# Where the folded down weights are stored, and where the first raw weights are placed, in a spectral layer with a gated feed-forward on one core

## The chip, the cores and the metric

The kernel runs on one core of a Trainium2 chip. The metric is the device time of one execution in microseconds, as the median of several runs. The core's engines are PE (matrix products), DVE (vector operations), ACT (activations and copies), POOL (a second, slower vector engine) and SP, whose queue issues most of the transfers. Each engine works through its own instructions strictly in order and waits at the head of its queue for whatever the next instruction needs.

## The reference

The input x has 4096 rows of 640 values. A modulation vector (six pieces of 640: sa, ca, ga, sb, cb, gb) is computed from c.

```python
mod = (_silu(c) @ w_mod).reshape(c.shape[0], 6, 1, -1)
h = _layernorm(x) * (1 + ca) + sa
x = x + ga * _A_ref(h, ...)          # FFT over the rows, a two-layer block-diagonal net, inverse FFT
h = _layernorm(x) * (1 + cb) + sb
x = x + gb * ((_silu(h @ w_gate) * (h @ w_up)) @ w_down)   # 640 -> 1728 -> 640
```

Everything is float32. The kernel keeps that accuracy by splitting an operand into a high and a low part and adding three products (high·high, high·low, low·high).

## The kernel before

The first 313 us compute the spectral layer A. The rest is the feed-forward layer, to which the change belongs. Its 32 groups of 128 rows are cut into six tiles t = 0 to 5 (`TL`, of 4, 4, 6, 6, 6 and 6 groups). For each tile PE runs a fixed list of stages `STG`: weight blocks of gate and up (`w`, 14 of them, n = 0 to 13) and, in between, the down products of six pairs of blocks (`d`, p = 0 to 5; the remainder p = 6, called `NPR`, is used together with p = 5).

The order of all other work is made by a planner in the kernel's Python code, when the program is built. PE's stages move the planner's clock `now` on by assumed durations. Every other piece of work is a `Step`: an engine letter (A for ACT, V for DVE, P for POOL, S for SP's queue, N for nothing), an assumed duration, a function that issues the instructions, the keys it depends on, the key it finishes, the places it takes (`use`) and the places it gives back (`free`). Steps stand in chains, and a chain's steps are issued strictly one after another. After every 0.3 us of assumed PE time `sweep` goes through all chains and issues each first step whose dependencies and places are planned to be there in time. A step on SP is planned to be issued 0.45 us after it is taken up, and its transfer to end 0.9 us + its duration + 0.9 us later, behind all transfers planned before it (`free["D"]`). Where the plan is early, the real engine waits at the instruction, and all that stands behind it on that engine waits too.

The chain `down_w` prepares the down weights. In tile 0, `prep_wd(0, p)` does for each p: `load` the raw block of 640 KB from `w_down` into the one place `wd`; `fold(0)` and `fold(1)` on POOL, which multiply it in place by the gate row gb (L1589); for each half the `high` part on ACT (L1594) into a place of `wdh` and the `low` part on DVE (L1598) into a place of `wdl` (two places each, given back when a down stage is through); and `store`, which writes the folded block to the scratch tensor `wdd` (L1601), from which later tiles load it (L1580) without folding. Before, `store` is the last step of the block and gives the place `wd` back; the next block's `load` takes it.

The raw gate and up blocks r (L1405) are loaded by `load_w`, the first three (n = 1, 2, 0) ahead of the first stage. Each is split into high parts (ACT, L1423) and low parts (DVE, L1426), and POOL makes differences of its quarters, `ts` (L1470), for later tiles. PE's first stage `first_g` uses weights that the spectral part has prepared already; beside it ACT and DVE split the first rows (L1887 to L1893). A row of the next tile goes through a chain of its own: loads of the spectral result `cr` and of `x` (L1638, L1634), a product with the gate row on POOL (L1650), a split (`chh`, `chl`, L1654 and L1657), an inverse transform on PE (L1667), statistics on DVE (L1678), scales on POOL (L1686 to L1689), the normalised row `xn` on ACT (L1698) and its transposes on PE (L1731).

`place` fixes at which address each kind of tile lies: addresses are given out in the order of the calls. The feed-forward's memory lies over that of the spectral part, so a first tile can be written only when the last reader of what lay there is through.

Of the kernel before, what the change touches and what calls it, by code (L numbers as in the profile page):

```python
# [6 lines left out]
F32 = mybir.dt.float32  # L7
# [6 lines left out]
P = 128  # L14
D = 640
S = 4096
# [155 lines left out]
def body(tc, x, w1, b1, w2, b2, wg, wu, wd, c, wm, k_fa, k_tb, k_tx, k_bm, k_bx, k_ga, k_ge, k_id, out, dbg=None):  # L172
# [4 lines left out]
    def f32(ap):  # L177
        return ap.bitcast(F32)
# [22 lines left out]
    with ExitStack() as top:  # L201
# [922 lines left out]
        with ExitStack() as ff:  # L1124
# [36 lines left out]
            free = dict.fromkeys("AVPSDG", 0.0)  # L1161
            done = {}
# [164 lines left out]
            def take(tag, shape, dt, bufs, name):  # L1327
                if tag == "wt":
                    turns[0] += 1
                    if turns[0] % 3 == 0:  # L1330
                        return low_p.tile(shape, dt, tag=tag, name=name)
                    bufs = 2
                if first.get(tag):
                    return first[tag].pop(0)
                return fp.tile(shape, dt, tag=tag, bufs=bufs, name=name)

            def place(tag, shape, dt, bufs, name):
                first.setdefault(tag, []).append(fp.tile(shape, dt, tag=tag, bufs=bufs, name=name))
# [6 lines left out]
            place("rb0", [P, 512], F32R, 1, "a13")  # L1345
            place("wt", [P, 2, 2, 2, P], F32R, 2, "wt0_0a")
            place("R", [P, 5, 256], F32, 2, "r0_2")
            ht0 = [fp.tile([P, 2, 512], F32R, tag=f"h{j}", bufs=1, name=f"ht0_{j}") for j in HT0]
            place("h0", [P, 4, 2, P], F32, 1, "ts0")
            place("h1", [P, 5, 256], F32, 1, "r0_1")  # L1350
            place("pc", [P, D], F32, 4, "cr0_0")
            place("px", [P, D], F32, 2, "x0_0")
            for f in range(2):
                for hl in range(2):
                    place(f"a{2 * f + hl}", [P, 512], F32R, 1, f"a0_0_{f}_{hl}")
            place("h32", [P, 5, 2, P], F32, 1, "h32_1_0")
            place("wd", [P, 2, D], F32, 1, "wdr0_0")
            place("wdh", [P, 2, D], F32R, 2, "wdh0_0")
            place("sg", [P, 512], F32, 4, "sg0_0_0")
            place("s", [P, 512], F32, 5, "hx0_0")  # L1360
# [30 lines left out]
            raw = {}  # L1391
# [6 lines left out]
            def load_w(t, n):  # L1398
                k, p = WG[n]
                tag = rtag(t, n)  # L1400

                def load():
                    r = raw[t, n] = take(tag, [P, 5, 256], F32, bufs[tag], f"r{t}_{n}")
                    if k in "gu":
                        nc.sync.dma_start(r, (wgv if k == "g" else wuv)[:, :, 256 * p:256 * p + 256])  # L1405
                    else:
                        c, f = (P, 12 * P) if k == "m" else (64, 13 * P)
                        nc.sync.dma_start(r[:, :, 0:c], wgv[:, :, f:f + c])
                        nc.sync.dma_start(r[:, :, c:2 * c], wuv[:, :, f:f + c])

                return Step("S", 2.1, load, key=("raw", t, n), use=(tag,))
# [86 lines left out]
            wds = {}  # L1498
# [74 lines left out]
            def prep_wd(t, p):  # L1573
                if t in DT:
                    return block_loads(t, p)

                def load():
                    w = wdraw[t, p] = take("wd", [P, 2, D], F32, 1, f"wdr{t}_{p}")
                    if t:
                        nc.sync.dma_start(w.rearrange("p a b -> p (a b)"), wdd[p])  # L1580
                    elif p < NPR:
                        nc.sync.dma_start(w, wd[256 * p:256 * p + 256, :].rearrange("(f p) d -> p f d", p=P))
                    else:
                        nc.sync.dma_start(w[:, 0], wd[12 * P:13 * P, :])
                        for h in range(2):
                            nc.sync.dma_start(w[64 * h:64 * h + 64, 1], wd[13 * P:F, :])

                def fold(f):
                    pool.tensor_tensor(wdraw[t, p][:, f], wdraw[t, p][:, f], gbb[0], op=OP.mult)  # L1589

                def high(f):
                    if f == 0:
                        wds[t, p] = [take(q, [P, 2, D], F32R, 2, f"{q}{t}_{p}") for q in ("wdh", "wdl")]
                    act.activation(wds[t, p][0][:, f], wdraw[t, p][:, f], AF.Copy)  # L1594

                def low(f):
                    h, l = wds[t, p]
                    dve.tensor_tensor(l[:, f], wdraw[t, p][:, f], f32(h[:, f]), op=OP.subtract)  # L1598

                def store():  # L1600
                    nc.sync.dma_start(wdd[p], wdraw[t, p].rearrange("p a b -> p (a b)"))  # L1601

                raw_ = ("wdr", t, p)
                out = [Step("S", 1.7, load, (("wds", p),) if t else (), raw_, ("wd",))]
                for f in range(2 if t == 0 else 0):
                    out += [Step("P", 1.65, lambda f=f: fold(f), (raw_, ("gbb", 0), ("gbb", 1)), ("wdg", p, f))]
                for f in range(2):
                    out += [Step("A", 0.74, lambda f=f: high(f), (raw_,) if t else (("wdg", p, f),), ("wdhh", t, p, f),
                                 () if f else ("wdh", "wdl")),
                            Step("V", 0.83, lambda f=f: low(f), (("wdhh", t, p, f),), ("wdf", t, p, f),  # L1610
                                 free=("wd",) if f and t else ())]

                if t == 0:
                    out.append(Step("S", 1.7, store, (("wdf", t, p, 0), ("wdf", t, p, 1)), ("wds", p), free=("wd",)))
                return out

            def wd_keys(t, p):
# [805 lines left out]
            for n in (1, 2, 0):  # L2423
                prep.add([load_w(0, n)])
                prep.run()
            for i in range(2):
                done["gbb", i] = done["wb", 0, 0, i] = 0.0

# [27 lines left out]
            for t in range(NT):  # L2456
                for p in (0, 1, NPR, 2, 3, 4, 5) if t in DT else range(NPR + 1):
                    down_w.add(prep_wd(t, p))
                if t >= NS:
                    for n in range(NW):  # L2460
                        if WG[n][0] != "s":
                            wtl.add([load_t(t, n, i) for i in range(2)])
                if t:
                    left_l.add(load_h(t))
                    x2_l.add(load_x2(t))
                    rows[t].add(row_chain(t))
# [55 lines left out]
```

## Time and profile before

| what | value |
|---|---|
| three timed runs | 1455.12, 1455.55, 1457.36 us, median 1455.55 |
| the profiled execution | 1462.3 us, its span 1460.5 us |
| mean granted clock of PE | 0.998 |
| PE busy | 1409.4 us, 97% of the span |
| DVE, ACT, POOL busy | 1091.5, 784.8, 537.9 us |
| HBM read, written | 264.04 MB, 104.86 MB |

All times of the profile are counted from the start of the span. A row of waits says which engine and line waited for which, how long in total, how often, and the longest. A row of a timeline begins with start and length. A row of the chain of work that ended last gives start, length and the work. "x6" counts instructions.

### The profile page before, as it was taken

What the parts mean: (1) busy time and instruction counts of PE and PEld (TensorE: products, weight loads), DVE (VectorE), ACT (ScalarE), POOL (GpSimd) and SP (SyncE); (2) the same over time, 40 slices, a digit from 0 to 9 for tenths busy, and PEclk for the clock granted to TensorE, in tenths of its full rate; (3) what the DMA queues carried; (4) which work ended last, traced back from release to release, by engine and by line L of the source; (5) the groups of instructions that cost most, each with busy time, mean ns of one, the idle gap of its engine ahead of it and who ended that gap; (6) DMA issues with size and microseconds to landing.
All of it is one profiled execution on the core that took longest, in us unless ns stands there. A gap on an engine that the chain in (4) does not pass through costs nothing.

```text
span 1460.5 us, 23931 instructions
## 1 busy us (share of the span) xinstructions
PE 1409.4 (97%) x8516; PEld 1329.9 (91%) x8516; DVE 1091.5 (75%) x1979; ACT 784.8 (54%) x1560; POOL 537.9 (37%) x640
## 2 busy tenths in 40 slices
PE   7999999999989989999999999999999999999998
PEld 2699999968879878899999999999999999999998
DVE  8878778869777888668878768788747767567775
ACT  7868878745454455545555456556434444244432
POOL 5300100146444234233444434534324545046532
PEclk9999999999999999999999999999999999999999
DMA  9987677647877977897886997888696666966652
GB/s 379 321 257 251 208 219 234 212 138 263 272 264 252 326 257 258 296 357 271 284 312 214 355 368 246 289 279 272 237 346 218 219 216 238 353 210 232 204 188 83
DMA packets 186807, 379.66 MB, mean 260 GB/s; under 512 B 22176, under 2 KB 104672, under 8 KB 184896
## 3 DMA queue, kind: packets, MB, share of 16 engines
q1 hardware_dynamic: 178496, 361.75, 72.2%
q0 software_dynamic: 6608, 13.77, 3.0%
q10 hardware_dynamic: 1584, 2.62, 0.5%
q8 instruction: 67, 1.10, 0.3%
q14 instruction: 52, 0.43, 0.1%
HBM read 264.04 MB, written 104.86 MB: 253 GB/s over the span
## 4 chain that ended last, share of the span: by engine, by line
PE 69%; DVE 11%; DMA 10%; ACT 4%; issue 2%; POOL 2%; SPq 1%; DVEq 0%; POOLq 0%; ACTq 0%
PE pd L2396 12%; PE pw L2075 7%; PE pw L2077 7%; PE pw L2076 7%; PE pd_X L2256 4%; PE pc L780 4%; PE pl L712 4%; DMA cr<-s 3%; PE pd_Y L2256 2%; PE pw L2086 2%; PE pw L2088 2%; PE pw L2087 2%; PE pg L1939 2%; PE pg L1940 2%; PE pg L1941 2%
## 5 line engine op out<-in xcount | busy, mean ns | idle before, releaser
L2396 PE MATMUL pd<-wdh,a 128*128 128x320 f32 x1040 | 240.2, 311 | 0.3 <-ACT sg L1961 0.3
L2396 PEld LDWEIGHTS pd<-wdh,a 128*128 128x128 f32 x1040 | 177.4, 189 | 0.9 <-ACT sg L1961 0.5
L1426 DVE TENSOR_TENSOR wb<-r,wb 128x512 fp32r<-128x512 f32 (+3 forms) x154 | 159.8, 1049 | 12.6 <-ACT wb L1423 10.4
L2396 PE MATMUL pd<-wdl,a 128*128 128x320 f32 x540 | 166.9, 310 | 0.0
L2075 PE MATMUL pw<-h,wt 128*128 128x384 f32 x416 | 141.2, 339 | 4.3 <-ACT s_x L2094 3.3
L2077 PE MATMUL pw<-h,wt 128*128 128x384 f32 x416 | 140.3, 337 | 0.0
L2076 PE MATMUL pw<-h,wt 128*128 128x384 f32 x416 | 139.7, 336 | 0.0
L2368 DVE TENSOR_TENSOR x<-x,pd 128x320 f32<-128x320 f32 x240 | 109.2, 478 | 38.3 <-PE pd L2396 34.3
L1423 ACT ACTIVATE wb<-r 128x512 fp32r<-128x512 f32 (+3 forms) x170 | 116.4, 704 | 30.7 <-PE pw L2088 23.3
L2075 PE MATMUL pw<-h,wb 128*128 128x384 f32 x312 | 105.2, 337 | 0.0
L2077 PE MATMUL pw<-h,wb 128*128 128x384 f32 x312 | 104.7, 336 | 0.0
L2076 PE MATMUL pw<-h,wb 128*128 128x384 f32 x312 | 104.6, 335 | 0.0
L1939 PE MATMUL pg<-ht,wb 128*128 128x512 f32 x260 | 102.8, 396 | 0.0
L1941 PE MATMUL pg<-ht,wb 128*128 128x512 f32 x260 | 101.7, 391 | 1.0 <-DVE wb L1426 1.0
L2396 PEld LDWEIGHTS pd<-wdl,a 128*128 128x128 f32 x540 | 102.0, 189 | 0.4
L1940 PE MATMUL pg<-ht,wb 128*128 128x512 f32 x260 | 101.7, 391 | 0.0
L2094 ACT ACTIVATE s_x<-pw 128x384 f32<-128x384 f32 x52 | 25.4, 489 | 114.0 <-PE pw L2077 113.3
L1650 POOL TENSOR_TENSOR cr<-cr,gab 128x640 f32<-128x640 f32 x28 | 47.5, 1697 | 101.4 <-DMA cr<-s 83.5
L2075 PEld LDWEIGHTS pw<-h,wt 128*128 128x128 f32 x416 | 78.1, 188 | 6.9 <-ACT s_x L2094 4.9
L842 POOL DMA_DIRECT2D s<-co x28 | 15.5, 555 | 181.9 <-ACT co L841 172.9
L2076 PEld LDWEIGHTS pw<-h,wt 128*128 128x128 f32 x416 | 78.2, 188 | 0.0
L2077 PEld LDWEIGHTS pw<-h,wt 128*128 128x128 f32 x416 | 78.1, 188 | 0.0
(353 smaller groups left out, 4049.5 us busy)
## 6 DMA issues: line engine op xcount, KB each, us to landing
wt<-td SPq DMA_DIRECT2D x104, 512.0 KB, 5.4
hs<-ho SPq DMA_DIRECT2D x52, 512.0 KB, 5.4
h<-hs SPq DMA_DIRECT2D x32, 768.0 KB, 8.5
r<-in_B_w_up_dram SPq DMA_DIRECT2D x36, 640.0 KB, 5.4
r<-in_B_w_gate_dram SPq DMA_DIRECT2D x36, 640.0 KB, 5.3
wdr<-wdd SPq DMA_DIRECT2D x21, 640.0 KB, 5.4
td<-wt SPq DMA_DIRECT2D x25, 512.0 KB, 5.7
g<-s SPq DMA_DIRECT2D x7, 1280.0 KB, 7.0
```

The costliest lines, as they stand in the source:

```text
L712: mm(pls[g][:, :NN], *seqs[g][i], start=(i == 0), stop=(i == n - 1))
L1423: act.activation(wbs[t, n][:, 0, ks, e], raw[t, n][:, ks, e], AF.Copy)
L1426: (pool if onp else dve).tensor_tensor(wbs[t, n][:, 1, ks, e], raw[t, n][:, ks, e], f32(wbs[t, n][:, 0, ks, e]), op=OP.subtract)
L1939: mm(b, wh, hh, start=(kk == 0), stop=False)
L1940: mm(b, wh, hl, start=False, stop=False)
L1941: mm(b, wl, hh, start=False, stop=(kk == 4))
L2075: mm(b, w(0, kp), a[:, kp, 0], start=start and kp == 0, stop=False, skip_group_check=not start)
L2076: mm(b, w(0, kp), a[:, kp, 1], start=False, stop=False, skip_group_check=not start)
L2077: mm(b, w(1, kp), a[:, kp, 0], start=False, stop=kp == 1, skip_group_check=not start)
L2256: mm(bk[b, i][:, :320], x, y, start=new and j == 0, stop=j == len(seq) - 1, skip_group_check=not new)
L2368: dve.tensor_tensor(x2[:, e], x2[:, e], x[0][:, :320], op=OP.add)
L2396: mm(pd[g, hf][0][:, :320], l, m, start=i == 0, stop=i == len(s) - 1 and not (last and len(gs) > 1))
```

## The change

Four edits. The store of a folded block becomes the fourth step of its block, right behind the second fold, with the two fold keys `("wdg", p, 0)` and `("wdg", p, 1)` as its dependencies in place of the low parts' keys; the high and low parts follow it in the chain. The place `wd` is given back by a new step of engine "N", which issues nothing and depends on the store's key and on the second low part. The place `h1` (the first raw up weights, `r0_1`) is given out ahead of the five tiles `ht0` in place of behind `h0`, and the place `wd` (the first raw down weights, `wdr0_0`) ahead of the tiles `a0` to `a3` in place of behind `h32`, which moves the tiles between by 5 to 6 KB per partition. And after the first three raw loads the planner is told that these blocks are there at time 0, and that SP's queue and the transfers are free at time 0.

```diff
             place("R", [P, 5, 256], F32, 2, "r0_2")
+            place("h1", [P, 5, 256], F32, 1, "r0_1")
             ht0 = [fp.tile([P, 2, 512], F32R, tag=f"h{j}", bufs=1, name=f"ht0_{j}") for j in HT0]
             place("h0", [P, 4, 2, P], F32, 1, "ts0")
-            place("h1", [P, 5, 256], F32, 1, "r0_1")
             place("pc", [P, D], F32, 4, "cr0_0")
             place("px", [P, D], F32, 2, "x0_0")
+            place("wd", [P, 2, D], F32, 1, "wdr0_0")
...
             place("h32", [P, 5, 2, P], F32, 1, "h32_1_0")
-            place("wd", [P, 2, D], F32, 1, "wdr0_0")
...
                 if t == 0:
-                    out.append(Step("S", 1.7, store, (("wdf", t, p, 0), ("wdf", t, p, 1)), ("wds", p), free=("wd",)))
+                    out.insert(3, Step("S", 1.7, store, (("wdg", p, 0), ("wdg", p, 1)), ("wds", p)))
+                    out.append(Step("N", 0.0, lambda: None, (("wds", p), ("wdf", t, p, 1)), free=("wd",)))
                 return out
...
             for n in (1, 2, 0):
                 prep.add([load_w(0, n)])
                 prep.run()
+                done["raw", 0, n] = 0.0
+            free["S"] = free["D"] = 0.0
```

## The prediction, made before the changed kernel was run

> **What bounds the kernel now.** I read the page first, then the waits of PE in the stretch that the edited steps fill, then the chain that ended last through it, then the granted clock around the largest wait.
>
> ```profile
> span 1460.5 us, 23931 instructions
> PE 1409.4 (97%) x8516; PEld 1329.9 (91%) x8516; DVE 1091.5 (75%) x1979; ACT 784.8 (54%) x1560; POOL 537.9 (37%) x640
> ```
>
> PE is busy for 97% of the span, so its 51.1 us of idle time (1460.5 - 1409.4) are all that a change of order can win. The folds lie between 313 and 460 us. The waits of PE there (total, times, longest):
>
> ```profile
> PE pt L1731 <- ACT xn L1698: 3.5, 1, 3.5
> PE py L1667 <- DVE chl L1657: 2.8, 2, 1.6
> PE pg L1901 <- DVE ht L1893: 0.7, 1, 0.7
> PE pg L1899 <- ACT ht L1887: 0.4, 1, 0.4
> PE pd L2396 <- ACT sg L1961: 0.3, 1, 0.3
> ```
>
> Together 7.7 us. None of them names a down weight. The chain shows what stands behind the largest:
>
> ```profile
> 391.90 6.00 DMA wdd<-wdr
> 397.92 6.88 DMA wdr<-in_B_w_down_dram
> 404.96 1.58 POOL wdr L1589
> 406.56 0.75 ACT wdh L1594
> 407.33 1.41 DVE wdl L1598
> 408.74 0.81 DVE st_b L1678 x2
> ```
>
> The reader is to see a ring with one buffer: the store of block p, the load of block p+1 into the same place, its fold, its high part, its low part. Only then does DVE come to the row statistics that were queued behind the low part, and PE waits 3.5 us for the normalised row made from them. The down weights themselves aren't late for PE; they hold up what is queued behind them. After that wait the clock falls (columns: length, PE, PEld, DVE, ACT, POOL busy, granted clock, DMA):
>
> ```profile
> 409.30:412.60 3.30, 0.10 (x1) 0.00 (x0) 3.27 (x7) 2.12 (x4) 2.49 (x5) 1.00 0.00 0
> 412.60:416.00 3.40, 3.13 (x13) 2.73 (x13) 2.07 (x2) 2.29 (x6) 3.32 (x4) 0.50 0.48 125
> 416.00:419.40 3.40, 3.40 (x23) 3.26 (x22) 1.64 (x5) 3.40 (x9) 0.11 (x1) 1.00 1.05 405
> ```
>
> At clock 0.50 PE starts 13 matmuls in 3.40 us, at 1.00 it starts 23 in the next 3.40. The dip costs (23 - 13)/23 x 3.4 = 1.5 us, so the whole wait is worth 3.5 + 1.5 = 5.0 us. The Trainium skill (TensorE: Matmul & The Clock Gate, What's actually happening) says that the clock halves after an idle window of about 3.4 us; this row agrees, and by its rule a wait shortened below that would win the dip as well.
>
> **The early store.** Before, the store of a block is handed to SP's queue behind both low parts; now it goes in behind the second fold. What that is worth is read from the transfers and from one block (start, length):
>
> ```profile
> wdd<-wdr SPq DMA_DIRECT2D x7, 640.0 KB, 7.1
> ...
> wdr<-in_B_w_down_dram SPq DMA_DIRECT2D x6, 640.0 KB, 6.6
> ```
> ```profile
> 344.75 3.56 POOL L1589 TENSOR_TENSOR wdr<-wdr,gbb 128x640 f32<-128x640 f32 x2 [5.14 <-DMA wdr<-in_B_w_down_dram]
> ```
> ```profile
> 354.96 0.51 SPq L1601 DMA_DIRECT2D wdd<-wdr  x1
> ...
> 362.83 0.38 SPq L1582 DMA_DIRECT2D wdr<-in_B_w_down_dram  x1
> ```
>
> The fold of block 1 ended at 344.75 + 3.56 = 348.3, its store was issued at 354.96, 6.6 us later, and the next load at 362.83. Who stood in this ring, between 313 and 460 us:
>
> ```profile
> SPq L1582 <- DMA wdd<-wdr: 6.1, 3, 2.6
> SPq L1584 <- DMA wdd<-wdr: 5.3, 1, 5.3
> SPq L1580 <- DMA wdd<-wdr: 5.1, 1, 5.1
> ```
> ```profile
> POOL wdr L1589 <- DMA wdr<-in_B_w_down_dram: 35.1, 6, 10.8
> ```
> ```profile
> ACT wdh L1594 <- POOL wdr L1589: 18.4, 11, 5.1
> ```
>
> SP stood 16.5 us in front of loads until the store had landed, POOL 35.1 us in front of folds, ACT 18.4 us in front of high parts. In the new order the high part of block p still has to wait for a place of wdh (two places, so for p of 2 and more until down stage p-2 is through), but load, fold and store no longer wait for that: they run one block ahead. The place of the raw weights comes free at the later of store and second low part. As the store now starts some 3 to 7 us earlier and lands while the parts wait for their place, the load finds it landed (the 16.5 us of SP go), and the high part finds its fold done (the 18.4 us of ACT go). With them go the 3.5 us of PE and their dip (5.0), the second wait for chl (2.8 - 1.6 = 1.2) and the 0.3 for sg: **-6.5 us**. The added step "N" issues nothing and costs nothing. No transfer is added: seven stores and seven loads, as before.
>
> What stays: a load lands after 6.6 us, while the plan counts 0.45 + 0.9 + 1.7 + 0.9 = 3.95. POOL is sent to the fold 2.65 us too early in each of six blocks, 16 us of the 35.1, and the row scales behind it are late by that. If PE felt this in the same proportion, 16/35.1 x 6.5 = 3.0 us would come back; if DVE and ACT being free covers it, nothing. I take **+1.1**, nearer to nothing, because in the chain above the way to PE ran through ACT and DVE.
>
> **The places and the plan's start.** With h1 ahead of the ht tiles and wd ahead of the a tiles, the first up weights lie over hidden-layer tiles of the spectral part and the first down weights over its second weight matrix (from the tile sizes, added up in order). Both were last read by these matmuls:
>
> ```profile
> 287.30 2.34 PE pc L780 x16
> ```
> ```profile
> 313.12 0.40 SPq L1405 DMA_DIRECT2D r<-in_B_w_up_dram  x1
> ```
> ```profile
> 304.00:312.00 8.00, 7.49 (x32) 4.86 (x32) 6.39 (x18) 2.75 (x5) 5.70 (x13) 1.00 0.00 0
> 316.00:324.00 8.00, 7.32 (x30) 5.46 (x31) 5.97 (x9) 6.26 (x10) 0.00 (x0) 1.00 1.08 383
> ```
>
> So the places are free at 289.6, not at 313, and the first loads can fill the 8 us in which DMA moved nothing, in place of the 8 us in which it was full. No PE wait hangs on these loads themselves. But the plan now holds the raw weights to be there at 0, and so four subtractions and two folds of POOL, which ran from 324 on, go in front: POOL, idle from 316 to 324 above, will work beside the first gate's low parts.
>
> ```profile
> 324.38 3.29 POOL L1589 TENSOR_TENSOR wdr<-wdr,gbb 128x640 f32<-128x640 f32 x2 [8.91 <-PE pg L1901]
> ```
> ```profile
> 329.76 0.73 POOL L1470 TENSOR_TENSOR ts<-r 128x256 f32<-128x256 f32 x1
> ```
> ```profile
> L1893 DVE TENSOR_TENSOR ht<-hx,ht x5: 691/692/694, 316.7 to 322.3; 128x512 fp32r<-128x512 f32 x5
> ```
> ```profile
> L1598 DVE TENSOR_TENSOR wdl<-wdr,wdh x56: 771/816/3174, 328.0 to 1034.5; 128x640 fp32r<-128x640 f32 x56
> ```
>
> The row of wdl gives the price: 816 ns in the median, 3174 ns for the one at 328.0 that ran beside POOL, a loss of 2.36 us. The five low parts L1893 ran without POOL at 692 ns and PE follows them closely (0.7 us of waiting). The moved POOL work is 3.29 + 4 x 0.73 = 6.2 us. Bounds: nothing, if it falls between the low parts; 5 x 6.2/6 = 5.2 us, if each of them waits for one POOL operation. I take **+2.4**, the loss in the row. The Trainium skill (GPSIMD Engine Reference, Key points) says that POOL shares its SBUF interfaces with VectorE and contends with operations that have two SBUF inputs; the row of wdl agrees. Against it stands the first wait for chl, **-1.6**, which came while DVE was behind because of the same work at 325 to 335. Bounds of the pair: -1.6 to +5.2.
>
> **The sum.** -6.5 + 1.1 + 2.4 - 1.6 = -4.6 us, on a profiled execution of 1462.3 us whose span is 1460.5. The three timed runs have a median of 1455.55, 6.75 below it; I take the difference over whole: 1455.55 - 4.6 = 1451.0 us.
>
> **The rivals.** *Later waits go too.* All steps behind are planned anew, the rows earlier than before. After 460 us PE still waits, among others:
>
> ```profile
> PE pt L1731 <- ACT xn L1698: 2.5, 1, 2.5
> PE pd_X L2256 <- DVE x L2230: 1.9, 2, 1.4
> PE py L1667 <- DVE chl L1657: 1.8, 1, 1.8
> PE pg L1941 <- DVE wb L1426: 1.0, 1, 1.0
> ```
>
> If the first, third and fourth went as well (5.3), it would be 1445.7. For it: they are of the same kind. Against: by then the folds are over.
>
> *The first gate pays.* If the low parts pay the full 5.2 beside POOL and the 3.0 come back, the sum is -6.5 + 3.0 + 5.2 - 1.6 = +0.1: no change, 1455.6. For it: the wdl row. Against: DVE has gaps there. The same time would come out if the change did not do what it says, the loads being held by the low parts as before.
>
> *The store holds SP's queue.* The store now waits on POOL's fold at the head of SP's queue, and if the fold is 2.65 us late, so is everything behind it: the raw loads, the row loads cr and x, the stores td and hs. Before, the store found the fold done. The raw loads have cover; a row that is late goes on to PE. Three such blocks cost 8.0, and one of the waits a dip of 1.5: -4.6 + 9.5 = +4.9, 1460.5. It decides from about two blocks on (4.6/2.65). For it: POOL is late in every block. Against: the row work is ahead by what SP and ACT have won.
>
> **How the numbers follow.** A measurement of this kernel can tell about 0.2% (2.9 us) from no change. Forecast 0.47, later waits go too 0.13: faster 0.60. First gate pays, or nothing happens: same 0.20. SP's queue held: slower 0.20. The forecast's own bounds are -8.1 (1447.5) and +1.6 (1457.2), from the ends above. The range takes in most of both outer cases: 1444.5 to 1460.0.
>
> **What would show it.** Right: the first raw loads issued near 301 us; the store within 1 us of the second fold's end; ACT's 18.4 us in front of wdh nearly gone, SP's 16.5 too; POOL's 35.1 halved; no dip of the clock near 412. The L1893 low parts longer than 692 ns, and PE's wait there 2 to 3 us. Wrong: SP standing on the fold for over 2 us in several blocks with PE waiting for chl or xn, or new waits of PE above 2 us after 460 us.

## The result, and the profile after

| kernel | median, us | range | runs |
|---|---|---|---|
| before, same chip | 1455.95 | 1455.12 to 1457.36 | 4 |
| after | 1464.7 | 1463.02 to 1466.28 | 4 |

The medians lie 8.8 us apart. The ratio on record, which is not their quotient, is 1.0051, 95% interval 1.0031 to 1.0071; by it the change makes the kernel slower by 7.4 us, where 4.6 us less was forecast. The per cents below, and the us worked out from them, go by such ratios. From L1615 on, lines of the changed kernel count one more than before. First the page of the profile after (its execution took 1463.56 us):

```profile
span 1461.8 us, 23933 instructions
PE 1412.9 (97%) x8516; PEld 1332.3 (91%) x8516; DVE 1104.2 (76%) x1979; ACT 785.9 (54%) x1560; POOL 540.2 (37%) x640
```

The profiled execution of before (1462.3 us) lay 6 us above its own timed runs, so the two pages side by side hide most of the loss. It has to be found by stages. The waits in the ring of the down weights, 313 to 460 us, first:

```profile
SPq L1601 <- POOL wdr L1589: 15.6, 5, 4.5
SPq L1601 <- DMA wdr<-in_B_w_down_dram: 12.1, 5, 4.7
SPq L1582 <- DMA wdd<-wdr: 2.6, 1, 2.6
ACT wdh L1594 <- POOL wdr L1589: 5.2, 2, 4.0
POOL wdr L1589 <- DMA wdr<-in_B_w_down_dram: 5.4, 3, 3.1
```

The ring does what the change says. SP's wait for the store's landing, 16.5 us before, is 2.6; ACT's wait for the fold fell from 18.4 to 5.2, POOL's for the raw block from 35.1 to 5.4. In their place SP now stands 27.7 us in front of the store itself. The first raw loads are issued from 298.4 us on, near the 301 of the forecast. Around 412 us (columns as in the prediction):

```profile
402.00:412.60 10.60, 10.60 (x59) 9.13 (x58) 9.62 (x20) 4.12 (x6) 3.43 (x8) 1.00 0.80 280
412.60:416.00 3.40, 3.40 (x21) 2.82 (x20) 1.71 (x3) 3.17 (x8) 1.10 (x1) 1.00 0.44 167
```

PE is busy throughout and the clock stays at 1.00: the wait of 3.5 us and its dip are gone, as forecast. But PE waits elsewhere. The longer waits of PE between 313 and 460 us, with the one for `chl`, and then all between 840 and 910 us, where before had none:

```profile
PE pg L1902 <- DVE ht L1894: 5.8, 2, 4.8
PE pt L1732 <- ACT xn L1699: 1.6, 1, 1.6
PE pd L2397 <- DVE x L2369: 1.2, 2, 0.9
PE py L1668 <- DVE chl L1658: 0.3, 1, 0.3
```
```profile
PE pw L2078 <- DVE wb L1426: 2.4, 1, 2.4
PE pw L2076 <- DVE x L2369: 1.4, 1, 1.4
```

The first loss, 5.8 us against 0.7, is in the first gate stage. The line of its low parts, what POOL did meanwhile (timeline: start, length), and the windows around it:

```profile
L1894 DVE TENSOR_TENSOR ht<-hx,ht x5: 679/693/6178, 318.6 to 329.0; 128x512 fp32r<-128x512 f32 x5
```
```profile
319.98 6.78 DVE L1894 TENSOR_TENSOR ht<-hx,ht 128x512 fp32r<-128x512 f32 x2 [0.29 <-ACT hx L1891]
```
```profile
319.68 0.75 POOL L1470 TENSOR_TENSOR ts<-r 128x256 f32<-128x256 f32 x1
320.37 0.75 POOL L1470 TENSOR_TENSOR ts<-r,ts 128x256 f32<-128x256 f32 x1
321.08 3.04 POOL L1589 TENSOR_TENSOR wdr<-wdr,gbb 128x640 f32<-128x640 f32 x2
324.07 1.52 POOL L1651 TENSOR_TENSOR cr<-cr,gab 128x640 f32<-128x640 f32 x1
```
```profile
319.90:326.70 6.80, 2.00 (x8) 1.34 (x9) 6.72 (x3) 3.97 (x7) 6.24 (x6) 1.00 0.71 212
326.70:330.10 3.40, 3.40 (x10) 2.61 (x9) 3.33 (x6) 0.00 (x0) 0.00 (x0) 0.51 0.17 39
330.10:333.50 3.40, 3.40 (x16) 2.74 (x16) 1.02 (x2) 0.92 (x2) 0.00 (x0) 1.00 0.32 36
```

One low part of 0.69 us took 6.18 us, from 319.98 to 326.15: it ended 0.56 us after the last of these products of POOL (325.59), which follow one another without a pause. Behind it the clock falls: 10 matmuls in 3.40 us against 16 in the next, (16 - 10)/16 x 3.4 = 1.3 us more. Both inputs and the output of this low part lie in SBUF, the memory of the kernel's tiles. The Trainium skill (SBUF — State Buffer, SBUF: two separate sides) calls the SBUF port pair of DVE and POOL an exclusive lock, held for a whole instruction, with the other side blocked. The blocking agrees; here it lasted over several instructions of POOL, not one.

### The profile page after: what moved, and what is told of

The parts are those of the page before. It is cut to its first block, busy times and chain, and to the rows that moved or that the text cites. A ratio compares the mean times of both kernels' runs of the same rounds, so it can differ in the third digit from the quotient of the medians.

```text
span 1461.8 us, 23933 instructions
## 1 busy us (share of the span) xinstructions
PE 1412.9 (97%) x8516; PEld 1332.3 (91%) x8516; DVE 1104.2 (76%) x1979; ACT 785.9 (54%) x1560; POOL 540.2 (37%) x640
## 4 chain that ended last, share of the span: by engine, by line
PE 64%; DVE 11%; issue 9%; DMA 7%; ACT 4%; POOL 3%; SPq 1%; POOLq 0%; ACTq 0%; DVEq 0%
PE pd L2397 11%; PE pw L2076 7%; PE pw L2078 7%; PE pw L2077 7%; PE pd_X L2257 4%; PE pg L1940 2%; PE pg L1941 2%; PE pg L1942 2%; PE pd_Y L2257 2%; DMA cr<-s 2%; DVE wb L1426 2%; PE pw L2087 2%; PE pw L2089 2%; PE pw L2088 2%; DVE ho L1773 2%
```

## The experiments

Before is 1455.8 to 1457.0 us in each comparison; the ratio is to the runs of before on the same chip.

### Each half alone

The store alone keeps the places and the plan's start of before; the places alone keep the old store.

> The early store and the step N alone; places and the plan's start as before. Theory 1 (the loss of the change is POOL's work moved beside the first gate's low parts; the early store is sound): faster than before by 2 to 7 us, PE's waits between 313 and 460 us down from 7.7 us to 1 to 3, PE's wait for the low part ht unchanged at 0.7 us. Theory 2 (the early store holds SP's queue, or replans the later stages to its cost): slower by 3 us or more, with PE waits for chl, xn or wb that before did not have, while the wait for ht stays 0.7.

> The two places moved and the plan's start at 0, the store as before. Theory 1: slower than before by 5 to 9 us, with a wait of PE for the low part ht of 4 to 6 us, a single L1893 of 5 us or more beside POOL's ts, fold and cr, and a clock dip of 3.4 us behind it. Theory 2: within 2 us of before.

The store alone: 1458.1 us, ratio 1.0015 (1.0001 to 1.0029), where it should have won. The places alone: 1452.4 us, 0.9979 (0.9962 to 0.9996). So the places with the plan's start, forecast to cost 0.8 us, win, and the store does not. Neither theory holds whole: the second had the store 3 us or more slower, and 2.2 were measured; the first had the places 5 to 9 us slower. Waits of PE with the store alone, the longest between 313 and 460 us and all between 840 and 910 us, and then with the places alone, the longest between 313 and 460 us:

```profile
PE py L1668 <- DVE chl L1658: 4.3, 2, 2.7
```
```profile
PE pw L2078 <- DVE wb L1426: 2.4, 1, 2.4
PE pw L2076 <- DVE x L2369: 2.2, 1, 2.2
```
```profile
PE pg L1901 <- DVE ht L1893: 5.7, 2, 4.8
```

The loss in the first gate belongs to the places, the waits of tile 3 to the store. Neither trace has a wait for `xn` between 313 and 460 us: the wait of 3.5 us at 409 us goes with the places alone as well as with the store alone. It cannot be won twice. With the store alone PE gains little from it, though: the wait for `chl` grew from 2.8 to 4.3 us, a dip came at 388 us in place of the one at 412, and all waits in this stretch add up to 6.7 us against 7.7 before.

### The first gate: how much POOL work, or how it is spaced

The whole change, with a tiny product on POOL in `first_g` that reads the last low part, so that POOL's later work starts behind the low parts:

```diff
+                pool.tensor_tensor(sc[:, 0:1], f32(ht0[4][:, 1, 0:1]), mone[:, :1], op=OP.mult)
```

> The whole change, and one POOL product of one column that reads the last low part of the first gate, so that POOL's ts and folds start behind it. Theory 1: PE's wait for ht back to 0.7 us, no dip near 327, 6 to 8 us faster than the change, and so at or below before (1450 to 1456). Theory 2: the wait for ht goes, but the time stays over 1460.

1462.54 us, ratio 1.0044 (1.0026 to 1.0061). All five low parts take 691 to 694 ns again and PE waits 0.7 us there, but further on it waits for the row, whose product on POOL now comes later:

```profile
PE py L1668 <- ACT chh L1655: 3.5, 1, 3.5
PE py L1668 <- DVE chl L1658: 2.9, 2, 1.7
```

So this moves the loss and does not end it. Next the kernel before with six products of no use put on POOL beside the low parts, four of 128x256 and two of 128x640, all writing the same columns, so that each waits for the one in front:

```diff
+                z = first["h0"][0].rearrange("p a b c -> p (a b c)")
+                for j in range(4):
+                    pool.tensor_tensor(z[:, 0:256], gab[:, 0:256], gab[:, 256:512], op=OP.mult)
+                for j in range(2):
+                    pool.tensor_tensor(z[:, 0:640], gab, gab, op=OP.mult)
```

> The kernel before with six added POOL products that nobody needs (four of 256 and two of 640 columns, 6.1 us by the rows of ts and fold), placed beside the first gate's low parts; their results are overwritten. Theory 1: one L1893 takes 5 us or more, PE waits for ht 4 to 6 us, a dip follows, 5 to 8 us slower than before. If POOL and DVE only take turns operation by operation: each of the low parts takes 1 to 1.7 us, PE waits 2 to 3 us, no dip, 1 to 3 us slower.

Nothing: 1455.56 us, 0.9993 (0.9978 to 1.0008). This falsified the expectation that POOL work beside the low parts is the cost by its amount alone. The twin has the same six products, each into columns of its own, so that none waits:

> The kernel before with six added POOL products again, the same sizes as in the first such run, but each writes columns of its own, so that none waits for the one ahead of it. Theory 1, refined (DVE gets the shared access only where POOL has a gap, which a wait on its own last result makes): one L1893 takes 4 to 6 us, PE waits for ht 4 us or more, a dip of 3.4 us or longer follows, 5 to 8 us slower than before. If the number of POOL products is what counts: as in the first such run, no L1893 above 1 us, within 2 us of before.

1460.26 us, 1.0025 (1.001 to 1.004): 3.6 us, less than the 5 to 8 expected, but with the wait and the dip that were expected. The low parts and POOL's four short products with waits, then the same without:

```profile
L1893 DVE TENSOR_TENSOR ht<-hx,ht x5: 693/834/903, 316.1 to 321.9; 128x512 fp32r<-128x512 f32 x5
...
314.92 3.83 POOL L1898 TENSOR_TENSOR ts<-gab 128x256 f32<-128x256 f32 x4
```
```profile
L1893 DVE TENSOR_TENSOR ht<-hx,ht x5: 677/692/4711, 316.8 to 324.9; 128x512 fp32r<-128x512 f32 x5
...
315.78 2.77 POOL L1899 TENSOR_TENSOR ts<-gab 128x256 f32<-128x256 f32 x4
...
PE pg L1907 <- DVE ht L1893: 4.7, 1, 4.7
```

The same four products on POOL, 3.83 us with small pauses or 2.77 us without: with pauses every low part gets in (at most 0.90 us), without them one is shut out for 4.71 us.

With the places moved but the plan's start left as before (the three lines of the last hunk taken out), less POOL work is beside the gate:

> The two places moved, the plan's start as before: every engine works through the same order as before, only the first loads are earlier. If the moved loads alone bring POOL beside the first gate: the two folds run there one behind the other, PE waits 1.5 to 3 us for ht, 0 to 3 us slower. If the plan's start is what counts (ts, folds and the row's product in one run of POOL): PE's wait for ht stays below 2, within 2 us of before, and the faster later stages of the run with places and plan's start are not there.

1456.51 us, 1.0008 (0.9995 to 1.002). The longest low part is 2.57 us here, beside two folds in a row, and PE waits 2.5 us, more than the 2 expected. PE, DVE, ACT and POOL have the order of before here, and the gain is gone: it needs the plan's start.

### Pauses on POOL, without and with the early store

A tiny product that reads the result just made, behind each of the first four `ts` and the first two folds, makes POOL pause:

```diff
+                        if n == 0:
+                            pool.tensor_tensor(sc[:, 0:1], s[:, o, 0, 0:1], mone[:, :1], op=OP.mult)
...
+                    if p == 0:
+                        pool.tensor_tensor(sc[:, 0:1], wdraw[t, p][:, f, 0:1], mone[:, :1], op=OP.mult)
```

In the whole change, and in the places alone:

> The whole change, and behind each of the first four ts and the first two folds a POOL product of one column that reads its result, so that POOL has a gap there. Theory 1, refined: no L1894 above 2 us, PE's wait for ht 0.7 to 2.5 us, no dip near 327, 4 to 8 us faster than the change (1457 to 1461), still above before because of the waits that the early store's plan has at 350 to 380 and near 880 us. If the first gate is not what the change pays for: the time stays at 1463 to 1466.

> Places and plan's start without the early store, with the same gaps on POOL. Theory 1, refined: PE's wait for ht falls from 5.7 to 0.7 to 2.5 us and the dip behind it goes; 4 to 7 us faster than the run with places and plan's start alone (1452.4), so 1445 to 1449, below before by 0.5 to 0.8%. If that run's gain has nothing to do with the first gate's time: 1451 to 1454.

The whole change: 1461.89 us, 1.0035 (1.0022 to 1.0049), short of the 4 to 8 us expected. The places alone: 1447.59 us, 0.9945 (0.993 to 0.996), which beats both kernels, and again, on another chip:

> The places and the plan's start moved, with the spacing products, a second time, beside the two others on one chip: 1447.6 us again within 3 us, that is below the kernel before by more than 0.2%.

1450.27 us, 0.9955 (0.9939 to 0.9971). A pause on POOL's timeline in the first of these, the low part that waited for it, and PE's wait:

```profile
315.66 0.72 POOL L1470 TENSOR_TENSOR ts<-r,ts 128x256 f32<-128x256 f32 x1
316.46 0.52 POOL L1472 TENSOR_TENSOR sc<-ts,mone 128x1 f32<-128x1 f32 x1
```
```profile
315.75 1.19 DVE L1897 TENSOR_TENSOR ht<-hx,ht 128x512 fp32r<-128x512 f32 x1 [2.79 <-ACT hx L1894]
```
```profile
PE pg L1905 <- DVE ht L1897: 1.4, 2, 1.1
```

A pause of 316.46 - 315.66 - 0.72 = 0.08 us is enough: the low part that began at 315.75 ends at 316.94, and PE waits 1.4 us in all in place of 5.7. That is worth 0.24 to 0.34% in the places alone (0.9979 against 0.9955 and 0.9945), 3.5 to 5 us; the intervals are apart for the second value only. In the whole change the intervals with and without pauses overlap: PE's wait at the gate falls from 5.8 to 1.3 us there, but others come behind it (2.2 for `xn`, 2.1 for `chl`), so that all waits between 313 and 460 us add up to 8.5 us against 9.8. There some 12 us are lost that the places alone do not lose (1.0035 against 0.9950, the mean of the two).

### The store itself, or the plan it makes

Moving the `Step` moves two things: the place of the transfer in SP's queue, and the planner's times, from which the order of all later work follows. The next pair takes them apart. In the first, the plan of the places alone with pauses keeps the late store, but the transfer is handed over by the step of the second fold:

```diff
-                    out += [Step("P", 1.65, lambda f=f: fold(f), ...
+                    out += [Step("P", 1.65, lambda f=f: (fold(f), store() if f else None), ...
...
-                    out.append(Step("S", 1.7, store, ...
+                    out.append(Step("S", 1.7, lambda: None, ...
```

> The places and the plan's start moved, with the spacing products, as in the run that took 1447.6 us; the plan still counts the store late, but the store is really handed to SP's queue behind the second fold. PE, DVE, ACT and POOL have the same instructions in the same order as in that run; SP's queue alone differs. If the loss of the early store comes from the changed order of the later steps (theory A): within 3 us of 1447.6, no wait of PE for wb or x between 840 and 910 us. If it comes from the store itself, on SP's queue or among the transfers (theory B): near 1461, the time of the whole change with spacing products (1461.9).

In the second, the plan of the whole change with pauses keeps its early step, which issues nothing, and the second low part's step hands the transfer over:

> The whole change with the spacing products (1461.9 us) and its plan, but the store is really handed to SP's queue behind the second low part, as in the kernel before. PE, DVE, ACT and POOL have the same instructions in the same order as in that run; SP's queue alone differs. Theory A (the order of the later steps): within 3 us of 1461.9, PE waiting for wb and x between 870 and 905 us with dips of the clock behind it. Theory B (the store itself): those waits are gone and the time is near 1448. Beside either, the folds should wait for the raw weights as in the kernel before, so it may be slower by some 2 us between 313 and 460 us.

| plan | store late | store early |
|---|---|---|
| of the late store | 0.9945, 0.9955 | 0.9951 (0.9934 to 0.9969), 1449.3 us |
| of the early store | 1.0061 (1.0047 to 1.0076), 1465.9 us | 1.0035 (1.0022 to 1.0049) |

Along the rows the real transfer moves and the order of PE, DVE, ACT and POOL is the same: the early store changes nothing that can be told in the one plan and gains about 0.26% in the other, where the two values come from two chips and their intervals just overlap. Down the columns only the plan differs: 0.8 to 1.2%. Both runs came out as theory A says, the second with 4.0 us above 1461.9 (3 were allowed, and some 2 for the folds). PE in the window 865 to 905 us, in before, in the plan of the late store with early transfer, and in the plan of the early store with late transfer:

```profile
865.00:905.00 40.00, 40.00 (x249) 39.98 (x248) 33.31 (x59) 25.90 (x53) 15.57 (x20) 1.00 0.81 280
```
```profile
865.00:905.00 40.00, 39.50 (x244) 39.17 (x243) 34.62 (x63) 24.55 (x54) 16.73 (x21) 1.00 0.80 272
```
```profile
865.00:905.00 40.00, 35.81 (x207) 34.91 (x206) 32.13 (x53) 20.30 (x44) 12.97 (x13) 0.96 0.86 289
```

PE's longest wait between 840 and 910 us is 0.5 us in the second; in the third it waits 2.4 us for `wb` and 1.8 for `x`. The waits of tile 3 stay with the plan. That also settles SP's queue. SP in the run with the plan of the late store and the early transfer, 313 to 460 us:

```profile
SPq L1605 <- POOL wdr L1591: 25.4, 7, 4.4
SPq L1605 <- DMA wdr<-in_B_w_down_dram: 19.7, 6, 6.4
```

SP stands 45.1 us in front of the store, more than the 27.7 of the changed kernel, and the kernel is as fast as with a late store.

### One step of the order

What in the plan costs? DVE's timeline in the whole change with pauses, ahead of PE's wait for `wb`:

```profile
871.38 0.68 DVE L1426 TENSOR_TENSOR wb<-r,wb 128x512 fp32r<-128x512 f32 x1
...
873.70 0.55 DVE L1915 TENSOR_TENSOR a<-sgr,a 64x384 fp32r<-64x384 f32 x1 [0.59 <-ACT a L1914]
874.27 0.96 DVE L1426 TENSOR_TENSOR wb<-r,wb 128x768 fp32r<-128x768 f32 x1
```

Between the two low parts of one weight block DVE does the products of the remainder block, and in them stands 0.59 us for ACT. PE needs the second part. So it was planned ahead of these products, in tile 3 alone (`rest`, before `mix_rem`):

```diff
+                    if t == 3:
+                        for key in wb_keys(t, n + 1):
+                            until(key)
                     x = done["act", t, 13, a] = mix_rem(b, N, a13, f"{t}_{a}")
```

> The whole change with the spacing products (1461.9 us); in tile 3 the second low part of the gate block behind the remainder block (DVE L1426, 128x768) is planned ahead of the remainder's two products on DVE instead of between them. Up to that place, at some 870 us, all engines have the same instructions in the same order; behind it the plan is made anew. If the order of DVE there makes PE's wait for wb (2.4 us and the dip of the clock behind it, 1.5): no wait for wb between 840 and 910 us, and the time some 4 us below 1461.9 as far as the new order behind it makes no waits of its own. If PE is merely ahead there and waits for whatever comes: another wait of over 2 us takes its place between 865 and 885 us, and the time stays within 2 us of 1461.9.

1453.37 us, 0.9977 (0.9961 to 0.9992): 0.58% or 8.4 us below the same kernel without these lines, and below the kernel before. The window, without them and with them, and the wait that is left:

```profile
865.00:905.00 40.00, 34.82 (x193) 33.91 (x193) 31.41 (x56) 17.58 (x38) 12.32 (x14) 0.91 0.75 252
```
```profile
865.00:905.00 40.00, 37.93 (x228) 36.98 (x227) 32.76 (x58) 19.87 (x41) 14.81 (x17) 1.00 0.85 273
```
```profile
PE pw L2082 <- DVE wb L1426: 1.9, 2, 1.4
```

193 matmuls become 228, and the two dips of the clock in this stage are gone. The wait for `wb` is shorter, not gone as expected (1.9 us in two): the first low part now begins 0.4 us behind POOL's product of the row (`cr`, 1.86 us from 870.52 on) and takes 2.03 us in place of 0.68. The wait of 2.8 us for `x` behind it is gone, since all behind that place was planned anew. So 8.4 us is what one moved step and the order that followed from it are worth, not that step's wait alone. Most of it lies in this stage: between 840 and 910 us PE's waits fall from 5.2 to 2.1 us, and with two dips of 1.3 us each (an estimate, from the first gate's dip) that makes 5.7 of the 7.1 us between the two profiled spans, 1460.7 and 1453.6 us.

## Why the prediction was wrong

Measured as ratios, each to before on its own chip, the way from before to after is: places and plan's start, with pauses on POOL and the transfer early, -0.49% (-7.1 us); the plan that the early step makes, +0.84% (+12.2, clear of the intervals); no pauses, +0.16% (+2.3, within the intervals): +0.51%, or 7.4 us.

**The step that failed: "All steps behind are planned anew".** It stood among the rivals, as a reason why waits could go; that they could come had no term in the sum and no place in the range, though new waits above 2 us after 460 us stood in the list of what would prove it wrong. They came, in tile 3, and the 12.2 us of the new order turned the sign. That the plan and not the transfer does it, the pair of queue experiments shows. That the order from tile 3 on is most of it, 8.4 us, the last experiment shows. The remaining 4 us (0.9977 against 0.9951) are open. In the trace of the last run and that of the plan of the late store with the early transfer, PE's waits add up to 8.0 against 6.0 us between 313 and 460 us, with one dip more at 436 us, to 5.7 against 6.0 between 460 and 840, and to 2.1 against 0.5 between 840 and 910; no run took these away.

**The early store, -6.5 + 1.1.** Its mechanism was right in the ring: ACT's, SP's and POOL's waits shrank as listed, the store landed sooner (median 3.5 us in place of 7.1), the gap at 409 us and its dip went. The step from the ring to PE was not: with the store alone PE's waits in this stretch fell by 1.0 us (7.7 to 6.7), because the wait for `chl` grew. With the orders held the early transfer is worth nothing that can be told (0.9951 against 0.9955 on the same chip and 0.9945 on another) in the one plan, 3.8 us (1.0035 against 1.0061) in the other. The term of 5.0 for the gap was credited to the store alone, but it goes with the places and the plan's start alone too, so it is in neither edit's gain when the other is there.

```profile
wdd<-wdr SPq DMA_DIRECT2D x7, 640.0 KB, 3.5
```

**The first gate, +2.4.** That POOL would work beside the low parts and PE would wait was right. The step that failed is the upper bound "if each of them waits for one POOL operation": one low part waited for five in a row, 6.18 us in place of 0.69, with a dip behind it. PE lost 5.8 - 0.7 + 1.3 = 6.4 us there, above the bound of 5.2. The row of `wdl` that set the 2.4 could have told it, read beside POOL's timeline of before:

```profile
328.02 3.17 DVE L1598 TENSOR_TENSOR wdl<-wdr,wdh 128x640 fp32r<-128x640 f32 x1
...
328.23 1.58 POOL L1650 TENSOR_TENSOR cr<-cr,gab 128x640 f32<-128x640 f32 x1
329.76 0.73 POOL L1470 TENSOR_TENSOR ts<-r 128x256 f32<-128x256 f32 x1
330.58 1.22 POOL L1470 TENSOR_TENSOR ts<-r,ts 128x256 f32<-128x256 f32 x1
```

It lasted over two operations of POOL, and ended at 331.19, 0.7 us after the end of the second (330.49), where POOL paused for 0.09 us.

**The plan's start** had no term of its own but the first gate's. With the pauses, it and the places win some 0.5%, although the moved loads alone, in the order of before, win nothing. The traces show where: behind 460 us PE's waits add up to 12.1 us with the order of before and the places moved, 7.0 of them for ACT's `s_z`, and to 7.2 us with the plan's start and the pauses as well, 1.0 of them for `s_z`. No run took these waits apart.

**The first wait for `chl`, -1.6**, went in the profile after (0.3 us left), but is back in other runs of the change (waits for `chl` of 2.9 us in all with the gate held, 2.1 with pauses): a term of one order, not of the edit.

**The dip rule.** The prediction took it that a wait shortened below about 3.4 us saves the dip as well. It does not: the wait for `wb` is 2.4 us, and behind it PE does 13 matmuls in 3.40 us at half the clock, though it was busy for 1.02 of the 3.40 us ahead of them. So the rule of the Trainium skill (TensorE: Matmul & The Clock Gate, What's actually happening), an idle window of about 3.4 us, is no safe lower bound for a wait here.

```profile
876.20:879.60 3.40, 1.02 (x6) 0.70 (x5) 2.56 (x5) 1.84 (x5) 0.00 (x0) 1.00 0.68 256
879.60:883.00 3.40, 3.40 (x13) 3.40 (x12) 2.99 (x5) 3.40 (x9) 1.34 (x2) 0.50 0.79 220
```

Nor does a longer wait always bring a dip. In the whole change with pauses PE waits 3.4 us for `chl` at 539 us, and the clock stays at 1.00 behind it:

```profile
539.20:542.60 3.40, 0.02 (x1) 0.00 (x0) 3.40 (x7) 0.00 (x0) 0.00 (x0) 1.00 1.05 387
542.60:546.00 3.40, 3.38 (x17) 2.94 (x18) 3.40 (x7) 2.29 (x4) 0.00 (x0) 1.00 0.98 247
```

So the length of a wait alone does not say whether its dip comes; what does, these runs do not show.

**The rivals.** "The store holds SP's queue" gave 1460.5, nearest to the result, by luck, for its reason is refuted: SP stands in front of the store and the time does not show it. "The first gate pays" had part of the loss. "Later waits go too" came true with the plan's start, and the other way round with the early step. A small slip: the upper bound of +1.6 comes to +1.7 from its terms (-6.5 + 3.0 + 5.2).

## What to carry to other kernels

Where a planner makes the order, an edit to one step is two changes, what the chip does and what the plan makes of it; hold one fixed to measure the other, and put a term of either sign for the new order into a forecast. Before a change is given up for its time, look where PE waits behind it: one step moved in tile 3, with the order that followed from it, was worth more than the change lost. Work moved onto POOL beside DVE operations with two SBUF inputs should not run without a pause while PE waits for them.

## What was not expected of the hardware

A DVE operation with two SBUF inputs got no turn while POOL's operations followed each other without a pause: 6.18 and 4.71 us for 0.69 us of work. The same POOL work with each operation waiting for the one in front left at most 0.90 us, so that POOL's slower, dependent sequence was the faster one for the kernel: 0.9993 (0.9978 to 1.0008) against 1.0025 (1.001 to 1.004).
